# Moving four output-projection matmuls of a decode kernel behind its last V pair, on one Trainium2 core

## The chip, the cores and the metric

The kernel runs on one core of one Trainium2 chip. The metric is the device time of one execution in microseconds (us). Every changed kernel was run beside the kernel before on the same chip. A time is the median of several executions; a trace tells of one of them. Two lengths occur: the time (about 1342.7 us) and the span of a trace from its first to its last instruction (about 1340.5 us); times within a trace count from the start of its span.

## The reference, cut to what matters

The program is one decode step of attention for 4 sequences and 32 heads over a cache of 8192 keys, with a small expert network beside it and a gate that mixes the two.

```python
q = (x @ wq) ...                                     # one token per sequence
scores = einsum("bhqd,bhkd->bhqk", q, k_cache) * Dh ** -0.5
p = softmax(scores)
o = einsum("bhqk,bhkd->bhqd", p, v_cache)            # k_cache and v_cache: 268 MB each
a = o.reshape(B, Sq, H * Dh) @ wo                    # wo: 4096 x 1024, 8 MB
b = ...                                              # gate, up, down of the expert network
return g * a + (1 - g) * b
```

Nearly all bytes are K and V, each read once.

## The kernel before

K and V stream through a ring of five slots, in "pairs" of 8 MB for four heads. SyncE issues all loads in program order; at most eight are under way, since each new issue waits for the landing of the one eight before it (the loads' landings use eight semaphores in turn; in the trace of before one of them has a landing at 1328.15, and the issue at 1328.21 is the next to use it). TensorE multiplies a V pair with 64 matmuls of 512 columns, ACT and DVE empty the sums (two ACT, three DVE instructions), and TensorE folds them into head outputs (8 small matmuls, "the fold", L625). `wo` comes in eight blocks of 1 MB with 8 matmuls each (four rows, two column halves), which add into `acc`.

```python
        # v_pair(d): the last pair comes in pieces, half 0 in two and half 1 in four
            for half, cuts in ((0, 1), (1, 2)) if d < ND - 1 else ((0, 2), (1, 4)):
                ...                                   # one dma_start per piece
        for u in range(4 * RD):                       # 16 x 4 matmuls
            ...
        # sum_up: 2 activations, 3 vector instructions, then finish() is put off to flush()

    def wo_block(g, r0=0, r1=FR, half=None):
        # ... one dma_start on SyncE, now
        def use():                                    # the matmuls, when it is called
            for r in range(r0, r1):
                for n in range(NH) if half is None else [half]:
                    mm_acc(n, LT[:, r, g, :], w[:, r, n * NB:(n + 1) * NB])
        return use

        # in the main loop
        if (kind, d) == ("v", ND - 1):
            for g in range(2):
                wo_block(g)()                         # wo 0 and 1 ahead of the last V pair
        if kind == "v":
            v_pair(d)
        # ...
    last = [wo_block(g) for g in range(2, 4)]
    # ... wo 4 to 6 in halves of 512 KB, wo 7 in three rows of 256 KB and two halves of 128 KB
    flush_sums()
    last.pop(0)()                                     # wo 2, while the V sums are emptied
    flush()                                           # the fold
    flush_late()
    last.pop(0)()                                     # wo 3
    o_rows(GE, NWB)
    for use in last:                                  # wo 4 to 7
        use()
```

## Time and profile before

| | before |
|---|---|
| median time, first three runs | 1342.71 us (1342.55 to 1342.71) |
| bytes read from HBM, mean rate | 575.68 MB, 429 GB/s |
| TensorE busy | 79% |
| last landing of a transfer | 1337.07 us |
| start of the last matmul | 1337.12 us |
| end of the span | 1340.5 us |

A landing is the moment at which all 16 marks of a transfer have reached its semaphore; the trace records it (those of the last transfer come from 1332.66 to 1337.07). The last matmul starts 0.05 us after the last landing, and some 3.4 us of matmul, copy, output write and closing follow. The lines of the page, the timeline and the chain of waits are shown in the prediction.

### The profile page before, as it was taken

Reading aid. Unit: us, or ns where it says so; the run is one execution under the profiler, and the core shown is the slowest. Engines: PE = TensorE matmul, PEld = TensorE weight load, DVE = VectorE, ACT = ScalarE, POOL = GpSimd, SP = SyncE. Lnnn points to the kernel's source line nnn. Section 1 sums busy time; section 2 is a strip of 40 time slices with the busy share of each in tenths; the row PEclk is TensorE's granted clock in tenths of the full one; section 3 lists DMA queues with packets and bytes.
Section 4 is the critical chain, followed back from the end, with each engine's and each line's share of the span. In section 5 each row is a group of like instructions: output and inputs, shape, how many; then the busy total and the mean of one; then the engine's idle time right before and its main releaser. Section 6 shows DMA issues by size and latency. Waiting matters only on the chain.

```text
span 1340.5 us, 6937 instructions
## 1 busy us (share of the span) xinstructions
PE 1065.4 (79%) x4654; PEld 141.1 (11%) x1422; DVE 638.4 (48%) x385; ACT 57.7 (4%) x58; POOL 66.5 (5%) x174
## 2 busy tenths in 40 slices
PE   2666877887778788787879778789697879889888
PEld 0101000001001010101001010101011011111111
DVE  2455988556544347554436256646145556100001
ACT  0000000100010000100010000100000000110000
POOL 2000000100010000100010000100001000100000
PEclk9787999898988998888989888889898989889889
DMA  9999999999999999999999999999999999999998
GB/s 415 433 436 435 437 434 427 435 432 430 437 433 429 441 427 427 440 432 432 437 431 431 432 437 438 425 432 427 438 436 438 430 422 434 434 430 429 428 427 346
DMA packets 15512, 576.14 MB, mean 430 GB/s; under 512 B 1740, under 2 KB 2004, under 8 KB 3170
## 3 DMA queue, kind: packets, MB, share of 16 engines
q1 hardware_dynamic: 15474, 575.69, 99.6%
q8 instruction: 24, 0.39, 0.1%
q14 instruction: 6, 0.05, 0.0%
q10 hardware_dynamic: 8, 0.00, 0.0%
HBM read 575.68 MB, written 0.01 MB: 429 GB/s over the span
## 4 chain that ended last, share of the span: by engine, by line
DMA 60%; DVE 23%; PE 14%; another core or an unknown queue 1%; issue 0%; ACT 0%; SPq 0%; DVEq 0%
DMA ring<-in_A_k_cache_dram 51%; DVE TB L494 21%; PE o_ps L579 9%; DMA ring<-in_A_v_cache_dram 8%; PE acc L287 2%; PE S_ps L499 2%; DVE OS L609 2%; DMA x<-in_gate_w_dram 2%; DVE mx L521 0%; PE o_ps L333 0%; PE S_ps L333 0%; PE led L625 0%; DVE PT L535 0%; ACT TB L530 0%
## 5 line engine op out<-in xcount | busy, mean ns | idle before, releaser
L494 DVE STREAM_TRANSPOSE TB<-ring 128x2048 uint32<-128x2048 uint32 x256 | 568.2, 2278 | 471.6 <-DMA ring<-in_A_k_cache_dram 464.6
L499 PE MATMUL S_ps<-TB,Z 128*128 128x512 bf16 x2048 | 531.3, 414 | 187.3 <-DVE TB L494 179.7
L579 PE MATMUL o_ps<-ring,PB 128*64 128x512 bf16 x2048 | 466.4, 390 | 45.7 <-DMA ring<-in_A_v_cache_dram 44.4
L499 PEld LDWEIGHTS <-Z 128*128 128x128 bf16 x512 | 52.9, 103 | 650.7 <-issue 650.7
L579 PEld LDWEIGHTS <-PB 128*64 128x64 bf16 x512 | 57.5, 112 | 447.0 <-issue 442.6
L617 DVE SCALAR_TENSOR_TENSOR OS<-o_ps,mE,OS 128x512 f32<-128x512 f32 x5 | 3.8, 751 | 136.7 <-ACT OS L615 136.7
L476 POOL COPY Z<-qa 32x4 bf16<-32x4 bf16 x128 | 25.6, 200 | 720.4 <-PE S_ps L499 695.0
L555 POOL COPY PB<-PT 32x1024 bf16<-32x1024 bf16 (+3 forms) x23 | 33.2, 1443 | 455.5 <-PE o_ps L579 350.1
L605 ACT ACTIVATE OS<-o_ps,mE 128x512 f32<-128x512 f32 x11 | 7.6, 687 | 673.4 <-PE o_ps L579 673.4
L553 ACT COPY PB<-PT 32x1024 bf16<-32x1024 bf16 (+3 forms) x21 | 30.3, 1442 | 22.5 <-PE o_ps L579 17.5
L609 DVE SCALAR_TENSOR_TENSOR OS<-o_ps,mE,OS 128x512 f32<-128x512 f32 x33 | 24.3, 737 | 1.5
L530 ACT ACTIVATE TB<-S_ps,mx 128x2048 bf16<-128x2048 f32 x4 | 7.9, 1967 | 321.4 <-DVE mx L527 321.4
L287 PE MATMUL acc<-ring,hT 128*4 128x512 bf16 x54 | 14.7, 444 | 5.4 <-ACT TB L530 5.4
L245 PE MATMUL S_ps<-identb,x 6*128 6x6 bf16 x8 | 0.6, 197 | 22.1 <-DMA x<-in_gate_w_dram 22.1
L333 PE MATMUL o_ps<-ring,xw 128*4 128x512 bf16 (+2 forms) x128 | 13.1, 496 | 5.2 <-DMA ring<-in_B_w_gate_dram 5.2
L287 PE MATMUL acc<-ring,LT 128*4 128x512 bf16 x64 | 14.6, 379 | 0.4 <-DVE LT L421 0.4
L625 PEld LDWEIGHTS o_ps<-selg,OS 128*128 128x128 f32 x88 | 11.5, 191 | 9.3 <-issue 8.9
L535 DVE STREAM_TRANSPOSE PT<-TB 128x2048 bf16<-128x2048 bf16 x4 | 9.2, 2312 | 6.4 <-ACT TB L530 6.4
L521 DVE TENSOR_REDUCE mx<-S_ps 128x1 f32<-128x2048 f32 x4 | 9.1, 2282 | 6.2 <-PE S_ps L499 6.2
L625 PE MATMUL o_ps<-selg,OS 128*128 128x8 f32 x88 | 10.5, 245 | 0.0
L615 ACT ACTIVATE OS<-o_ps,mE 128x512 f32<-128x512 f32 x5 | 3.4, 687 | 149.3 <-PE o_ps L579 149.3
L637 DVE SCALAR_TENSOR_TENSOR OT<-led,sgb,rinv 128x8 bf16<-128x8 f32 x5 | 1.2, 237 | 17.3 <-PE led L625 17.3
(83 smaller groups left out, 89.0 us busy)
## 6 DMA issues: line engine op xcount, KB each, us to landing
ring<-in_A_v_cache_dram SPq DMA_DIRECT2D x18, 4096.0 KB, 28.9
ring<-in_A_k_cache_dram SPq DMA_DIRECT2D x14, 4096.0 KB, 33.5
ring<-in_A_v_cache_dram SPq DMA_DIRECT2D x6, 2048.0 KB, 36.8
ring<-in_B_w_gate_dram SPq DMA_DIRECT2D x1, 7168.0 KB
ring<-in_B_w_up_dram SPq DMA_DIRECT2D x1, 7168.0 KB, 37.0
ring<-in_B_w_down_dram SPq DMA_DIRECT2D x1, 6912.0 KB
ring<-in_A_wo_dram SPq DMA_DIRECT2D x4, 1024.0 KB, 32.5
ring<-in_A_v_cache_dram SPq DMA_DIRECT2D x4, 1024.0 KB, 36.0
```

The lines of the kernel that those rows point to most:

```text
L287: nc.tensor.matmul(acc(n), lhsT=lhsT, rhs=rhs, start=start, stop=True, skip_group_check=True)
L333: nc.tensor.matmul(ps[32 * k:32 * k + Bn, z, :].rearrange("p (f r) -> p f r", r=FR)[:, :, lo:hi], lhsT=xT[TW * half + t], rhs=rhs, start=( ...
L476: nc.gpsimd.tensor_copy(out=Z[at, :, QP - 1 + QP * q], in_=qa[at, :, h0 + q, b])
L494: nc.vector.transpose(out=flat_t.bitcast(U32).rearrange("p (j i) -> p j i", j=CJ), in_=kn[:, half].bitcast(U32))
L499: nc.tensor.matmul(sps[:, z, :], lhsT=Z[:, 2 * half + e, s:s + P], rhs=T[:, 16 * z:16 * z + 16, :, e], start=(t + n + half + e == 0), stop ...
L521: nc.vector.tensor_reduce(out=mx[:, 0:1], in_=sps[:].rearrange("p z n -> p (z n)"), axis=AX.X, op=ALU.max)
L535: nc.vector.transpose(out=PT[:].rearrange("p j i -> p (j i)"), in_=PTs)
L553: nc.scalar.copy(out=Bv[at, :, :, q, :], in_=Pv[at])
L555: nc.gpsimd.tensor_copy(out=Bv[at, :, :, q, :], in_=Pv[at])
L579: nc.tensor.matmul(o_ps[w // 2][row:row + NM, w % 2, :], lhsT=PB[:, RD * (d % NW) + n, z].rearrange("p w s j -> p (w s j)"), rhs=vn[:, j0 ...
L609: nc.vector.scalar_tensor_tensor(out=OS[:], in0=o_ps[w // 2][:, w % 2, :], scalar=mE[:, w:w + 1], in1=OS[:], op0=ALU.mult, op1=ALU.add)
L625: nc.tensor.matmul(oT, lhsT=OS[:, q * Dh:(q + 1) * Dh], rhs=selg[:, q].rearrange("p t s -> p (t s)"), start=(q == 0), stop=(q == 3), skip_ ...
```

## The change: its intent, and the diff

In the trace of before TensorE stands still for 0.70 us ahead of the fold, because wo 2 gives it less work (8 matmuls, 1.89 us) than the emptying of the sums takes (2.87 us from 1324.44). The change takes rows 2 and 3 of wo 1 from before the last V pair and puts them there, so that the V pair can start earlier and the hole is filled.

```diff
-        def use():
-            for r in range(r0, r1):
+        def use(lo=r0, hi=r1):
+            for r in range(lo, hi):
...
         if (kind, d) == ("v", ND - 1):
-            for g in range(2):
-                wo_block(g)()
+            wo_block(0)()
+            near = wo_block(1)
+            near(0, 2)
+            last = [lambda: near(2, FR)]
...
-    last = [wo_block(g) for g in range(2, 4)]
+    last += [wo_block(g) for g in range(2, 4)]
...
     flush_sums()
-    last.pop(0)()
+    for _ in range(2):
+        last.pop(0)()
     flush()
```

## The prediction

> **What bounds the kernel now.** I read the page first: how full the transfers are, and whether anything else is.
>
> ```profile
> PE 1065.4 (79%) x4654; PEld 141.1 (11%) x1422; DVE 638.4 (48%) x385; ACT 57.7 (4%) x58; POOL 66.5 (5%) x174
> ...
> DMA 9999999999999999999999999999999999999998
> ...
> HBM read 575.68 MB, written 0.01 MB: 429 GB/s over the span
> ```
>
> The DMA row is full in all 40 slices; no engine comes near. Data arrives at 429 GB/s from start to end, and only what follows the last byte can be cut without fewer bytes. So I read the tail next, in the timeline of the engines (start, duration, engine, line).
>
> ```profile
> 1307.29 3.62 PE L287 MATMUL acc<-ring,LT 128*4 128x512 bf16 x16 [0.41 <-DVE LT L421]
> ...
> 1310.84 14.00 PE L579 MATMUL o_ps<-ring,PB 128*64 128x512 bf16 x64
> ...
> 1324.77 1.89 PE L287 MATMUL acc<-ring,LT 128*4 128x512 bf16 x8
> ...
> 1326.61 0.69 DVE L619 TENSOR_TENSOR OS<-OS,TB 128x512 f32<-128x512 f32 x1
> ...
> 1327.35 1.06 PE L625 MATMUL led<-selg,OS 128*128 128x8 f32 x8 [0.70 <-DVE OS L619]
> 1328.34 1.89 PE L287 MATMUL acc<-ring,LT 128*4 128x512 bf16 x8
> ...
> 1330.18 0.38 PE L287 MATMUL acc<-ring,LT 128*4 128x512 bf16 x1
> ```
>
> Here is wo 0 and 1 (16 matmuls), the last V pair (64), wo 2 (8), a hole of 0.70 us that waits for the V sums, their fold (L625), wo 3 (8), and from 1330.18 wo 4 to 7. The chain of waits makes this look like TensorE's tail:
>
> ```profile
> 1330.40 6.02 PE acc L287 x27
> 1336.42 0.04 issue
> 1336.46 1.05 PE acc L287 x4
> 1337.51 0.02 issue
> 1337.53 0.57 ACT TB L686
> ```
>
> The 0.04 us called "issue" is the important line. The DMA view of single issues (KB, us to landing) tells when the last wo pieces come in; their issues are at 1328.21, 1329.49 and 1330.76 in the queue's timeline.
>
> ```profile
> ring<-in_A_wo_dram SPq DMA_DIRECT2D x1, 256.0 KB, 8.2
> ring<-in_A_wo_dram SPq DMA_DIRECT2D x1, 128.0 KB, 7.3
> ring<-in_A_wo_dram SPq DMA_DIRECT2D x1, 128.0 KB, 6.3
> ```
>
> They land at 1328.21 + 8.2 = 1336.4, 1329.49 + 7.3 = 1336.8 and 1330.76 + 6.3 = 1337.1. The matmul that needs the first starts at 1336.46, the one that needs the last at 1337.12 (timeline of TensorE at that point): each some 0.05 us after its landing. So the end is set by the last transfer, not by TensorE; TensorE happens to arrive at the same moment.
>
> [...] 64 V matmuls in 14.00 us with a last one of 0.38 are 13.62 / 63 = 0.216 us. [...] before the last V pairs TensorE ran at 0.427 us per matmul until 1296, and the granted clock is 1.00 in every stretch after that. [...]
>
> **The change, part by part.** It moves four matmuls (rows 2 and 3 of wo 1, two column halves each) from before the last V pair to behind it. The order of instructions on TensorE shows this: 12 wo matmuls, 64 V, 4 + 8 wo, fold, wo 3, the rest as before. Nothing is added or removed: same matmuls, weight loads, transfers, in the same queue order with the same waits. ACT, DVE and POOL are the same.
> 1. The last V pair starts 4 x 0.216 = 0.86 us earlier, at 1309.97 instead of 1310.84. Its data must be there. The first piece landed by 1307.08, the next by 1311.98, the third by 1314.46 (the queue's issues of wo 4 and 5 wait for these landings and follow at once); later ones land 2.5 us apart, the last by 1321.92. TensorE needs the second 16 matmuls on (1313.4), the third 32 on (1316.9), the last 56 on: 1309.97 + 56 x 0.216 = 1322.07. All are in, the last by only 0.15 us. The full shift holds.
> 2. The V sums (two ACT, three DVE instructions) start 0.86 earlier and end at 1327.31 - 0.86 = 1326.45.
> 3. TensorE has 12 instead of 8 matmuls in that time: from 1323.91, 12 x 0.216 = 2.59, to 1326.50. wo 2 must be in when they reach it (1324.77): the queue's issue at 1324.41 waited for its landing, so it is. The fold can start at 1326.50 instead of 1327.35. The hole of 0.70 is gone, and I gain 0.85 us here (0.70 of hole, plus the part of the last wo matmul's modelled end that overlaps).
> 4. wo 3 starts at 1327.49 instead of 1328.34; it landed by 1326.93 (the next issue waits for it). wo 4 then starts at 1329.33 instead of 1330.18.
> 5. Now TensorE eats faster than the pieces come. A 512 KB piece is four matmuls, 0.86 us, but the pieces land 1.28 us apart: 1328.2, 1329.4, 1330.7 from the single issues, and, estimated at the same spacing, 1332.0, 1333.2, 1334.5. Before, TensorE began them at 1330.18, 1331.04, 1331.91, 1332.77, 1333.63, 1334.50: a lead of the data of 2.0, 1.6, 1.2, 0.8, 0.4 and 0.0 us. With 0.85 us taken off the start, the first three still begin 0.85 earlier, the fourth 0.7 or 0.8 earlier, the fifth some 0.35, the sixth not at all. The gain is used up at wo 6, second half.
> 6. The last five pieces (wo 7) land as before, up to 1337.1. Sum on the path that sets the end: 0.0 us. Of 0.85 us gained on TensorE, 0.85 becomes waits for transfers.
>
> After the last landing comes the same matmul (0.38), the copy (0.57) and the write. The prediction is 1342.6 us, the time before less at most a tenth for executions in which TensorE came a little late.
>
> **Rivals.**
> (a) TensorE sets the end, as the chain of waits shows it: 10 of its last 15 us are matmuls. Then the 0.70 to 0.85 us come off the time: 1341.9. For it: the chain, and hardly any gap. Against it: the landings above, and the last matmuls starting 0.05 us after them. It could hold in part in an execution where the clock comes back later than 1296 and TensorE is late; the three times of before, 0.16 us apart, show no such execution. I give it one in ten.
> (b) The new idle time drops the clock. If half clock came back at about 1334, a matmul would take 0.427 and the last twelve or so 0.21 us more each: 1345. For it: the four new holes of up to 0.4 us. Against it: I add up 0.04 + 0.4 + 0.35 + 0.2, some 1.0 us idle within 3.4 us. The windows view has TensorE busy 2.70 of 3.40 us at 1326.0 to 1329.4 with clock 1.00 kept, and the last drop, at about 1285.7, came after 3.41 us in which it was busy 1.35, 2.06 idle. One in thirty.
> (c) The last V piece comes late for the earlier pair (margin 0.15 us), so part of the shift is lost and a hole opens in the V pair. It would make 0 to 0.3 us on TensorE and nothing at the end, since step 5 hides it. The time stays 1342.6.
> (d) Transfers start earlier because buffers come free earlier. Against it: all wo issues from 1307 on follow the landing of the transfer eight back, which no matmul releases. No gain.
>
> **Range and chances.** The centre is 1342.6. Rival (a) pulls the low side to 1341.9, and executions of before differ by 0.16 us; another set of runs may lie some tenths off, so I put the ends at 1341.9 and 1343.3. A change by 2% is 27 us, over thirty times the whole hole. Nothing in the trace can make that: within 2% is 0.98, and I leave 0.01 for either side.
>
> **What would show it.** Right: no hole ahead of the fold; V pair about 1309.97, fold about 1326.5, wo 4 about 1329.3; then waits for the transfers of wo on TensorE between 1332 and 1334.5, about 0.8 us together; the last landings at the same time after the start of the span, the last matmul 0.05 us after the last landing. Wrong: a span shorter by 0.5 us or more with equal landings (then TensorE had bound), matmuls of 0.63 us in the last 5 us (clock), or last landings that move by more than the noise (transfers do depend on TensorE).

The forecast's sum is 0.0 us on the path that sets the end, so 1342.71 us less at most a tenth, 1342.6. The 0.216 us of steps 1 and 3 is the trace's own (13.62 / 63). The 0.427 us of rival (b) and the 0.63 us near the end are the spacing and the duration (634 ns) of V matmuls at half clock in the trace of before, between 1288 and 1295. The 3.4 us of rival (b) is the length of the stretches that I read in the windows view; how much idle time within such a stretch brings the clock down was not shown, so that the new holes leave it up was my estimate.

## The result, and the profile after

The changed kernel took 1342.80 us (median of 6, 1342.41 to 1343.62) beside 1342.71 us for the kernel before (6 runs, 1342.44 to 1342.99). The ratio is 1.0002, with a 95% interval of 0.9989 to 1.0015: the same. A ratio is the mean time of one kernel's runs over that of the other's of the same rounds, so it is not quite the ratio of the medians.

The page of the changed kernel has the same full DMA row and the same rate:

```profile
DMA  9999999999999999999999999999999999999998
...
HBM read 575.68 MB, written 0.01 MB: 429 GB/s over the span
```

The timeline of TensorE in the changed kernel (start, duration, engine, line; idle time before it and what ended it in brackets):

```profile
1304.23 2.75 PE L287 MATMUL acc<-ring,LT 128*4 128x512 bf16 x12 [0.41 <-DVE LT L421]
1308.01 3.61 PE L579 MATMUL o_ps<-ring,PB 128*64 128x512 bf16 x16 [1.03 <-DMA ring<-in_A_v_cache_dram]
1312.91 7.07 PE L579 MATMUL o_ps<-ring,PB 128*64 128x512 bf16 x32 [1.29 <-DMA ring<-in_A_v_cache_dram]
...
1322.85 1.89 PE L579 MATMUL o_ps<-ring,PB 128*64 128x512 bf16 x8 [0.60 <-DMA ring<-in_A_v_cache_dram]
1324.67 2.75 PE L287 MATMUL acc<-ring,LT 128*4 128x512 bf16 x12
1327.35 1.06 PE L625 MATMUL led<-selg,OS 128*128 128x8 f32 x8
...
1334.21 1.02 PE L287 MATMUL acc<-ring,LT 128*4 128x512 bf16 x4 [0.23 <-DMA ring<-in_A_wo_dram]
1335.44 2.95 PE L287 MATMUL acc<-ring,LT 128*4 128x512 bf16 x12 [0.21 <-DMA ring<-in_A_wo_dram]
```

The order is as intended: 12 wo matmuls, the V pair, 12 wo matmuls, and the fold without a hole. But the fold starts at 1327.35, to a hundredth where it was before. The V pair, which ran in one stretch of 14.00 us before, now waits four times for V transfers (3.3 us in all), and TensorE waits for wo pieces near the end. The chain of waits (start, duration, what) puts that into words:

```profile
1298.19 24.62 DMA ring<-in_A_v_cache_dram
...
1322.87 12.53 DMA ring<-in_A_wo_dram
...
1337.33 0.03 issue
1337.36 1.05 PE acc L287 x4
```

Where the chain of before named TensorE for its last 10 us, this one names transfers up to 1335.40. The last two wo issues in the queue's timeline, and the last one's landing in the DMA view of that issue alone:

```profile
1330.45 1.60 SPq L435 DMA_DIRECT2D ring<-in_A_wo_dram  x2
```

```profile
ring<-in_A_wo_dram SPq DMA_DIRECT2D x1, 128.0 KB, 6.2
```

The last issue starts 0.33 us before the end of that row, at 1331.72, and lands 6.2 us later; the record has 1337.98. The last matmul starts at 1338.02. So in both kernels the last matmul starts 0.04 or 0.05 us after the last landing. The two last matmuls in the timelines, the kernel before first:

```profile
1337.12 0.38 PE L287 MATMUL acc<-ring,LT 128*4 128x512 bf16 x1
```

```profile
1338.02 0.38 PE L287 MATMUL acc<-ring,LT 128*4 128x512 bf16 x1
```

Two things differ between these traces that the change did not make. First, the landings are 0.9 us later, and so is the end of the span (1341.4 against 1340.5). The queue was as late at the first wo issue, 1261.08 against 1260.13, long before anything that the change touches. Second, the clock. The windows view of both kernels around the pair before the last (us, busy time and count of PE, PEld, DVE, ACT, POOL, then granted clock, DMA share, GB/s), before first:

```profile
1285.65:1289.06 3.41, 1.53 (x4) 0.30 (x2) 0.40 (x1) 0.00 (x0) 0.00 (x0) 0.50 0.96 408
1289.07:1295.89 6.82, 6.82 (x21) 2.13 (x11) 0.24 (x1) 0.00 (x0) 0.00 (x0) 0.50 0.99 419
```

```profile
1285.65:1289.06 3.41, 0.59 (x3) 0.11 (x1) 1.32 (x2) 0.00 (x0) 0.00 (x0) 1.00 0.98 418
1289.07:1295.89 6.82, 6.82 (x36) 1.73 (x15) 0.24 (x1) 0.00 (x0) 0.00 (x0) 1.00 1.01 426
```

TensorE stands still for 3.9 us in both, but in the trace of before the clock fell to a half at 1285.65 and came back at 1295.89, and in this one it stayed full: 36 matmuls in the stretch that had 21, and V matmuls 0.216 us apart instead of 0.427. What told the two apart was not shown. In the trace of before TensorE was busy 1.35 us in the 3.41 us ahead of the drop (1282.24 to 1285.65); in the changed kernel it was busy 0.00 us in the 3.41 us from 1285.05, and the clock was 1.00 in them and after them. So how long TensorE stood still in such a stretch did not by itself decide it. At full clock TensorE ended the pair before the last 3.1 us earlier (its last matmul at 1303.17 against 1306.24) and arrived at the last V pair too early for its data. The experiments must hold the clock apart from the change.

### The profile page after: what moved, and what is told of

Its sections match the earlier page's. It is cut to its first block, busy times and chain, and to the rows that moved or that the text cites. A ratio compares the mean times of both kernels' runs of the same rounds, so it can differ in the third digit from the quotient of the medians.

```text
span 1341.4 us, 6879 instructions
## 1 busy us (share of the span) xinstructions
PE 1057.1 (79%) x4596; PEld 140.4 (10%) x1422; DVE 638.4 (48%) x385; ACT 57.7 (4%) x58; POOL 67.0 (5%) x174
## 4 chain that ended last, share of the span: by engine, by line
DMA 63%; DVE 22%; PE 12%; another core or an unknown queue 1%; issue 1%; ACT 0%; SPq 0%; DVEq 0%
DMA ring<-in_A_k_cache_dram 51%; DVE TB L494 20%; DMA ring<-in_A_v_cache_dram 9%; PE o_ps L579 8%; PE S_ps L499 2%; DVE OS L609 2%; PE acc L287 2%; DMA x<-in_gate_w_dram 2%; DMA ring<-in_A_wo_dram 1%; DVE mx L521 0%; PE o_ps L333 0%; PE S_ps L333 0%; DVE PT L535 0%; ACT TB L530 0%
## 5 line engine op out<-in xcount | busy, mean ns | idle before, releaser
L499 PE MATMUL S_ps<-TB,Z 128*128 128x512 bf16 x1990 | 524.7, 413 | 194.1 <-DVE TB L494 179.7
L625 PEld LDWEIGHTS o_ps<-selg,OS 128*128 128x128 f32 x88 | 11.5, 191 | 9.3 <-issue 8.8
L625 PE MATMUL o_ps<-selg,OS 128*128 128x8 f32 x88 | 10.5, 245 | 0.0
```

The lines of the kernel that those rows point to most:

```text
L499: nc.tensor.matmul(sps[:, z, :], lhsT=Z[:, 2 * half + e, s:s + P], rhs=T[:, 16 * z:16 * z + 16, :, e], start=(t + n + half + e == 0), stop ...
L625: nc.tensor.matmul(oT, lhsT=OS[:, q * Dh:(q + 1) * Dh], rhs=selg[:, q].rearrange("p t s -> p (t s)"), start=(q == 0), stop=(q == 3), skip_ ...
```

## The experiments

The theory: the end is set by the last transfer; TensorE has about 1 us in hand or less; and what the change gives depends on whether TensorE comes late to the last V pair. The rivals: TensorE sets the end; or the removed hole is always worth its length. The twelve runs fall into three sets, each with five rounds (one run has four executions). In sets 2 and 3 the kernel before had a median near 1343.0 us on another chip (1342.56 to 1343.84); in set 1 it was 1342.68 (1342.51 to 1344.05).

### Set 1: second traces, less and more work on TensorE

**Unchanged copies of both kernels.**

> An unchanged copy of the kernel before, for the noise and for a second trace. Both theories: the same time within 0.3 us of the median. What it tells is the trace: the two traces so far differ in the TensorE clock of the last V pairs (half clock from 1286 to 1296 before, full clock after the change), so the pair of traces is no comparison of the change alone. If this trace has full clock there, the theory that the last V pair then waits for its transfers expects its last 8 matmuls within 0.1 us of the last V landing, a hole of 0.7 to 0.8 us ahead of the fold all the same, and the fold about 4.5 us after that landing, just as in the changed kernel. If it has half clock, the tail of the first trace again.

> An unchanged copy of the changed kernel, for the noise and a second trace. The same time within 0.3 us of the median of the kernel before. At full clock: the last 8 V matmuls within 0.1 us of the last V landing, the fold about 4.5 us after it with no hole. At half clock: V pair without waits, no hole, fold 0.85 us earlier against the last V landing than the first trace of before.

The copy of before took 1342.71 us (ratio 1.0000, interval 0.9987 to 1.0012), that of the changed kernel 1342.86 (1.0002, 0.9989 to 1.0016). Single runs reached 1343.9 and 1344.0, so the scatter is larger than I had expected; the medians are within 0.2 us. Both traces have half clock somewhere between 1286 and 1297, for 6.8 and 10.2 us (the first eight V matmuls of the pair before the last took 2.74 us in the copy of before, and 1.89 at full clock in the first trace of the changed kernel), so neither shows the full-clock case. The copy of before shows a third form of its tail (timeline of TensorE, wo 2 and the fold):

```profile
1324.41 1.89 PE L287 MATMUL acc<-ring,LT 128*4 128x512 bf16 x8 [0.30 <-DMA ring<-in_A_wo_dram]
1326.62 1.06 PE L625 MATMUL led<-selg,OS 128*128 128x8 f32 x8 [0.33 <-DVE OS L619]
```

Here TensorE was earlier, stood 0.30 us waiting for wo 2 to land, and only the rest of the hole was left. The hole of 0.70 us was thus not a fixed thing of the kernel: part of it can be a wait for wo 2. The copy of the changed kernel has neither (fold at 1326.94, no wait), and its last matmul starts at 1337.30, 0.05 us after its last landing at 1337.25. Against the last V landing its fold is 0.61 us earlier than in the first trace of before (4.88 against 5.49), where 0.85 had been expected; counted from the last matmul of the pair before the last, it is 0.76 us earlier (20.354 against 21.117). The rest is that TensorE came 0.14 us later against that landing than in the first trace.

**Less work on TensorE**: the changed kernel without the matmuls of wo 3.

```diff
     flush_late()
-    last.pop(0)()
+    last.pop(0)
     o_rows(GE, NWB)
```

> The changed kernel without the 8 matmuls of wo 3 behind the fold; its transfer is still made. The result is wrong on purpose. TensorE is 1.73 us less busy behind the last V pair (8 x 0.216). Theory that the last transfer sets the end: 0.0 us, within 0.3, and TensorE's waits for wo pieces grow by about 1.7 us. Rival that TensorE sets the end: 1.7 us faster.

It took 1343.21 us (ratio 1.0001, 0.9989 to 1.0014). The result, wrong by design, still passed the comparison: this block's share of the output is below its tolerance. TensorE began wo 4 at 1329.10 instead of 1330.19, its waits for the later wo pieces, counted as start gaps above 0.216 us, grew from 1.1 to 2.2 us (2.8 had been expected: wo 4 began only 1.09 us earlier, since part of the time saved became a wait, 0.33 us of it for the folded outputs), and the chain names transfers nearly to the end:

```profile
1329.12 8.20 DMA ring<-in_A_wo_dram
1337.33 0.04 issue
```

1.73 us less work on TensorE gave nothing; 1.7 us less time would have been a ratio of 0.9987, just outside the interval, and the last matmul still starts 0.05 us after the last landing. This rejects the rival that TensorE sets the end, for executions like this one.

**More work on TensorE**: 16 matmuls of a zero weight ahead of wo 3.

```diff
+    def idle_mms(k):
+        for i in range(k):
+            mm_acc(i % NH, Zt[0][:, 0, 0:Bn], wo_home[0][:, 0, 0, (i % NH) * NB:(i % NH + 1) * NB])
...
     flush_late()
+    idle_mms(16)
     last.pop(0)()
     o_rows(GE, NWB)
```

> The changed kernel with 16 matmuls of a zero weight added between the fold and wo 3, 3.45 us of TensorE (16 x 0.216); the result stays right. In the changed kernel's trace TensorE's waits for wo pieces after the fold sum to 1.1 us (start gaps above 0.216 us: 0.18 + 0.39 + 0.37 + 0.19). Theory that transfers set the end with this little in hand: the waits vanish and the rest shows, 3.45 - 1.1 = 2.3 us slower. Rival that TensorE sets the end: 3.45 us slower. Rival that transfers have much in hand: 0.

It took 1345.39 us, 2.7 us over the kernel before and 2.5 over the copy of the changed kernel (ratio to before 1.0018, 1.0005 to 1.0031, too wide to tell 2.3 us from 3.45). The trace can: in it the last matmul starts at 1339.70, 2.37 us after the last landing at 1337.33. That is the expected 2.3 us, with all waits for wo gone. So TensorE has about 1.1 us in hand behind the fold when it was on time there, and no more.

### Set 2: TensorE late, and one transfer fewer

**TensorE late**: 24 zero-weight matmuls ahead of the wo blocks in front of the last V pair, in both kernels. The edit of the kernel before (of the changed kernel likewise):

```diff
         if (kind, d) == ("v", ND - 1):
-            for g in range(2):
-                wo_block(g)()
+            wo0 = wo_block(0)
+            idle_mms(24)
+            wo0()
+            wo_block(1)()
```

> The kernel before with 24 matmuls of a zero weight put in front of the wo blocks ahead of the last V pair, 5.18 us of TensorE, so that TensorE comes late to the last V pair whatever the clock did earlier; the result stays right. Expected: no waits for transfers in the last V pair, the hole of 0.7 us ahead of the fold, no waits for wo pieces, and an end set by TensorE: at full clock 5.18 less 2.4 us in hand at the V pair, less some 1.1 us in the wo pieces, so 1.6 us slower than the kernel before; at half clock up to 4.9 us slower.

> The changed kernel with the same 24 matmuls in the same place. Theory that the prediction's steps 1 to 4 hold where TensorE comes late: no hole, and 0.85 us less than the kernel before with the same 24 matmuls, both in the trace from the V pair on and in the time, at equal clock. Rival that the four moved matmuls give nothing even then: equal times of the two.

The medians are 1346.93 us (1344.11 to 1347.47) in the order of before and 1344.39 (1343.97 to 1345.58) in the changed order; ratios 1.0023 (1.0010 to 1.0035) and 1.0011 (0.9999 to 1.0024). A gap of 2.5 us is three times what was expected, though the intervals overlap. The traces show another size. From the last matmul of the pair before the last, which is the point where the two orders part, to the last matmul of the kernel, it is 1303.99 to 1339.21, or 35.22 us, against 1304.66 to 1339.12, or 34.46 us: 0.76 us. To the fold it is 25.70 against 24.94, the same 0.76. The executions behind a median may have had different clocks ahead of the last V pair. This was not shown: without a trace only the mean clock of a whole execution is on record, and that (0.908 to 0.915) does not set the long ones apart. Set 3 was made for this.

**One transfer fewer**: wo 2 is not loaded, and its matmuls read wo 1, in both kernels.

```diff
-        w = wo_home[home][:, at]
-        if half is None:
+        w = wo_home[home][:, 1 if g == 2 else at]
+        if g == 2:
+            pass
+        elif half is None:
```

> The kernel before without the transfer of wo 2 (1 MB); its matmuls use wo 1's rows instead, so the result is wrong on purpose and TensorE's work is the same. 1 MB at 429 GB/s is 2.44 us, so all wo pieces behind it land that much earlier against the last V landing. Theory that the transfers set the end with about 1 us in hand on TensorE: 1.1 us faster at full clock (0.3 at half clock), then TensorE sets the end and its waits for wo pieces are gone. Rival that TensorE sets the end: 0. Rival that transfers alone count: 2.4 us faster.

> The changed kernel without the transfer of wo 2, in the same way; the result is wrong on purpose. Here TensorE sets the end, from the last V landing on. If TensorE was on time for the last V pair (full clock), both orders fold as soon as the V sums are ready, so the change gives nothing even with TensorE as the bound: the same as the kernel before with this edit, within 0.2 us, 1.1 us faster than the kernel before. If TensorE was late (half clock): 0.85 us faster than the kernel before with this edit.

They took 1341.94 us (1341.63 to 1342.54) and 1341.35 us (1341.16 to 1341.85), 1.08 and 1.67 us below the kernel before; the ratios are 0.9993 (0.9979 to 1.0006) and 0.9988 (0.9975 to 1.0000). TensorE now sets the end: the last matmul starts 1.26 us after the last landing in the first and 0.54 us in the second. Of 2.44 us of transfer removed (1 MB at the 429 GB/s of the page) only 1.1 came out in the order of before, as expected. The interval is too wide to tell 1.1 us from 0 or 2.4, but the trace agrees: counted from the last V landing, the last landing came 2.51 us earlier than in the trace of before (12.70 against 15.21) and the last matmul 1.30 us (13.96 against 15.26). The fold in both timelines, the order of before first (L627 and L621 are L625 and L619 of the kernel before, moved by two added lines):

```profile
1326.98 1.06 PE L627 MATMUL led<-selg,OS 128*128 128x8 f32 x8 [0.70 <-DVE OS L621]
```

```profile
1326.63 1.06 PE L627 MATMUL led<-selg,OS 128*128 128x8 f32 x8
```

One has the whole hole, the other none. Yet measured from the last V landing (1322.53 and 1322.09) the fold comes 4.45 us after it with the hole and 4.54 us after it without. Filling the hole did not bring the fold forward, and the last matmul comes 14.06 us after the last V landing, against 13.96 in the order of before. In these two executions the order of instructions thus gave nothing: they lie 0.48 us apart, and 0.44 of it is the last V landing. The medians lie 0.59 us apart, where at most 0.2 had been expected, and this stays open. One rival is untested: in the executions without a trace TensorE may have come late, where the change does give time (set 3). The intervals overlap.

### Set 3: the clock held up

16 zero-weight matmuls fill TensorE's idle time ahead of the pair before the last, to keep the clock from dropping there; two kernels have 32 more ahead of the last V pair. The clock fell to half somewhere between 1284 and 1290 in nine of the ten traces without these matmuls, and in none of the four with them. The first eight V matmuls of that pair took 2.74 to 3.59 us in eight of the nine (the ninth is the copy of the changed kernel, with its 10.2 us of half clock), and 1.89 us in the other five.

```diff
+        if (kind, d) == ("v", ND - 2):
+            idle_mms(16, qa[:].rearrange("p e h b -> p (e h b)"))
         if kind == "v":
             v_pair(d)
```

> The kernel before with 16 matmuls of a zero weight in TensorE's idle 3.9 us ahead of the pair before the last (16 x 0.216 = 3.45 us), so that the clock does not drop there; the result stays right. Expected trace: clock 1.00 from about 1272 to the end, the last V pair waiting for its transfers, a hole of 0.7 us ahead of the fold, and the fold about 4.5 us after the last V landing. Time: the same as the kernel before within 0.3 us if the transfers set the end; up to 0.9 us faster if the late executions of the kernel before came from the clock.

> The changed kernel with the same 16 matmuls. Expected trace: V pair waiting for transfers, no hole, and the fold about 4.55 us after the last V landing, so 0.1 us later against that landing than in the other order: the hole is gone and nothing is gained by it. Time equal to the other order within 0.3 us. Rival that the removed hole is worth its length: 0.7 us faster.

They took 1342.77 us (1342.64 to 1344.45; ratio 1.0001, 0.9987 to 1.0014) and 1342.90 us (four runs, 1342.71 to 1343.92; 1.0000, 0.9987 to 1.0014). In both traces the clock is full from 1284 at the latest to the last matmul (the last 56 V matmuls of the pair before the last take 12.27 us in both, 0.216 us each), and the V pair waits for its transfers (2.4 and 3.3 us). The fold is 4.45 us after the last V landing in the order of before and 4.54 us in the changed order, as expected. One thing was not: in the order of before only 0.03 us of hole is left, since TensorE had waited 0.60 us for wo 2 first. Keeping the clock up gave no time either. The traced execution of the order of before, at full clock from 1284 on, took 1343.65 us, with its last landing at 1338.15: so a later stream, and not a dropped clock here, made this one long.

> The kernel before with the 16 matmuls that keep the clock up, and 32 more (6.91 us) ahead of the wo blocks in front of the last V pair, so that TensorE is late by a known amount in every execution. With 24 and a clock near full the last matmul came 35.2 us after the end of the pair before the last; with 32 it should come 36.95 us after it, at about 1340.2, some 2.6 us slower than the kernel before, with a spread below 1 us (it was 3.4 us without the 16).

> The changed kernel with the same 16 and 32 matmuls. With TensorE late in every execution by the same amount, the change should be worth what the traces with 24 show from the pair before the last to the fold, 25.70 - 24.94 = 0.76 us: 0.76 us faster than the other order with the same edit, in the time too. Rival, from the medians with 24 (1346.9 and 1344.4): 2.5 us. Rival that it gives nothing: 0.

The medians are 1345.02 us (1344.83 to 1347.07) and 1344.03 us (1343.68 to 1345.74): 0.99 us apart, with ratios of 1.0018 (1.0005 to 1.0032) and 1.0011 (0.9999 to 1.0024). The first is 2.1 us over the kernel before, where 2.6 had been expected, and the spread did not fall below 1 us. The traces decide the size. First zero-weight matmul, and the matmuls of wo 4 to 7 that end the kernel (all but the first of them), in the order of before:

```profile
1303.24 0.38 PE L287 MATMUL acc<-ring,Z 128*4 128x512 bf16 x1
...
1333.25 6.85 PE L287 MATMUL acc<-ring,LT 128*4 128x512 bf16 x31
```

and in the changed order:

```profile
1302.86 0.38 PE L287 MATMUL acc<-ring,Z 128*4 128x512 bf16 x1
...
1332.11 6.85 PE L287 MATMUL acc<-ring,LT 128*4 128x512 bf16 x31
```

From one to the other it is 30.01 us before and 29.25 us changed: 0.76 us, the same as with 24. The last matmuls lie 36.94 and 36.18 us after the pair before the last; 36.95 had been expected of the first. With TensorE late and at full clock the change is worth 0.76 us on TensorE, and with TensorE also setting the end this reaches the time; the intervals of the times are too wide to check the size. The 2.5 us of set 2 did not return.

### The tails in one table

Landings and starts in us, from the traces. "Last 8" is the start of the last 8 V matmuls, the first that need the last V piece.

| kernel | last V landing | last 8 | idle just ahead of the fold | fold | fold after last 8 | last landing | last matmul |
|---|---|---|---|---|---|---|---|
| before | 1321.86 | 1322.95 | 0.70 | 1327.35 | 4.40 | 1337.07 | 1337.12 |
| before, copy | 1321.87 | 1322.21 | 0.33 | 1326.62 | 4.41 | 1337.10 | 1337.14 |
| before, clock held up | 1323.00 | 1323.05 | 0.03 | 1327.45 | 4.40 | 1338.15 | 1338.19 |
| before, late by 32 | 1322.48 | 1325.80 | 0.70 | 1330.20 | 4.40 | 1337.67 | 1339.72 |
| changed | 1322.81 | 1322.85 | 0 | 1327.35 | 4.50 | 1337.98 | 1338.02 |
| changed, copy | 1322.06 | 1322.43 | 0 | 1326.94 | 4.51 | 1337.25 | 1337.30 |
| changed, clock held up | 1322.29 | 1322.33 | 0 | 1326.83 | 4.50 | 1337.46 | 1337.51 |
| changed, late by 32 | 1322.07 | 1324.56 | 0 | 1329.06 | 4.50 | 1337.41 | 1338.58 |

The column "fold after last 8" does not depend on the execution: 4.40 us in the order of before and 4.50 in the changed one, to 0.01 us. The six traces that are not in the table agree (4.40 twice, 4.50 four times). The way from the last V matmuls through the sums to the fold has one length, whether TensorE stands in a hole or works in it; the changed order adds 0.10, because its twelfth wo matmul ends just after the sums are ready (in the first trace of the changed kernel the sums end at 1327.20, that matmul starts at 1327.04 and ends at 1327.42). What the change can move is the column "last 8", by the 0.86 us of the four matmuls, and only where TensorE comes later than the last V landing. Net that is 0.76 us where TensorE is late, and a loss of 0.1 us where it is not. In the six kernels of the table that are not "late by 32" the last matmul starts 0.04 or 0.05 us after the last landing, whatever the fold did.

## Why the prediction was right or wrong

The time was right: 1342.6 us predicted, 1342.80 measured, inside 1341.9 to 1343.3. It rests on the bound and on step 6 alone, and these held for the reason given. What TensorE gains in steps 1 to 4 cancels before the end, so the hit says nothing for these steps, and they were in part wrong.

- **The bound and the "issue" line** were right. The last matmul follows the last landing in all six traces of kernels that were neither given late work nor spared a transfer, and in the kernel with 1.73 us less work on TensorE. Reading 0.04 us of "issue" as the end of a transfer was the step that mattered.
- **Step 1** (V pair 0.86 us earlier) was right only for a TensorE as late as in the first trace. The copy of the changed kernel, at half clock, shows it: its V pair starts 3.74 us after the pair before the last, against 4.60 in the first trace of before. In the first trace of the changed kernel the V pair instead waited 3.3 us. The step took the clock of one trace for the kernel's, with a margin of 0.15 us at the last piece; one execution with full clock overthrew it.
- **Step 2** follows step 1. The length of the sums did not change.
- **Step 3** was mis-sized. It counted 12 x 0.216 = 2.59 us to the fold and a gain of 0.85. The last wo matmul and the first of the fold start 0.31 us apart (1327.04 and 1327.35), not 0.216, as do the last V matmul and the first wo matmul (1324.36 and 1324.67); why was not shown. So the gain is 0.86 - 0.10 = 0.76, as the late kernels measured. In the prediction's terms, the "modelled end that overlaps" was the wrong term. And "the hole is gone" was not the source of the gain: the hole ends with the sums, and filling it moves nothing by itself.
- **Step 4** follows, with 0.76 in place of 0.85 where TensorE is late; at full clock nothing.
- **Step 5** was right in kind. In the changed kernel the wo pieces made TensorE wait, by start gaps of 0.18, 0.39 and 0.37 us ahead of the last three 512 KB pieces, 0.94 us in all, where the prediction had about 0.8. This is no proof of the change: the unchanged copy of before, with TensorE earlier than in the first trace, waited 0.80 us for the same pieces. The zero-weight matmuls measured the slack: 3.45 us added, 2.37 us shown.
- **Step 6** was right: no gain at the end.
- **Rival (a)** is rejected by the kernel with less work on TensorE. **(b)** did not occur: clock 1.00 to the last matmul. **(c)** occurred in a larger form than I gave it, 3.3 us instead of 0 to 0.3, and from another cause, the full clock and not the earlier pair; the end did hide it as it said. **(d)** did not occur: from the first wo issue to the last landing it is 76.94 us before and 76.90 changed.
- **The checks that I named** were of mixed use. The V pair at 1309.97, the fold at 1326.5 and wo 4 at 1329.3 were all missed (1308.01, 1327.35, 1330.19), because absolute places mix the clock and the stream's own drift of 0.9 us with the change. The last landings did move by more than I called noise, but the queue was already that late at 1261. The check of the last matmul against the last landing held.
- **A loose reading in the prediction.** The granted clock is 0.96 and not 1.00 in its last stretch (1337.50 to 1340.50), after the last matmul.

Open: what decides whether the clock falls ahead of the pair before the last, what makes single executions of many kernels here 1 to 2 us longer, why the late kernels of set 2 had medians 2.5 us apart, and why those without wo 2 differ by 0.59.

## What to carry to other kernels

Before filling a hole on an engine, ask what ends it: if it ends with another engine's result, work put into the hole is only worth the time that its old place gives back, and only if that place was on the path to that result. When transfers and an engine end within a microsecond of each other, look for the landing behind every short wait before believing the chain of waits. Measure distances within a trace from the last common event, and take a second trace of each kernel before comparing two.
